# Sliding-window attention and a residual MLP on one core: every transpose of q, k and u on TensorE in place of DMA transposes

## The chip, the core and the metric

The kernel runs on one core of a Trainium2 chip. A core has five engines with instruction streams of their own: TensorE (PE, matrix products and transposes), VectorE (DVE), ScalarE (ACT), GpSimd (POOL) and SyncE (SP, which here only issues DMAs). They meet through semaphores. Data lie in SBUF (128 partitions) and, as results of TensorE, in PSUM banks. DMAs, issued from the queues of SP, ACT and POOL, move data between the device's memory and SBUF, or within SBUF. The metric is device time in microseconds (us), the median of several runs; lower is better.

## The reference

Inputs are q, k, v of shape (4, 8, 768, 64) (batch, head, position, head dimension) and the parameters of an MLP with d_model 512 and hidden width 2048.

```python
# attention: 4 sink positions and a causal window of 128
scores = scale * np.matmul(q, k.transpose(0, 1, 3, 2))
keep = is_sink | in_window
scores = np.where(keep, scores, -1000000000.0)
a = softmax(scores)
x = np.matmul(a, v)               # heads side by side: (4, 768, 512)
# residual MLP with affine norms
a1 = alpha1 * x + beta1
tok = np.einsum('ts,bsd->btd', w_tok, a1)
u = x + lam * tok
a2 = alpha2 * u + beta2
ch = np.maximum(a2 @ w_ch1, 0.0) @ w_ch2
out = u + lam * ch
```

Two transposes of data are needed in each batch. The scores contract over the head dimension, so q and k are wanted with the head dimension on the partitions. The product a2 @ w_ch1 contracts over channels, so u is wanted with channels on the partitions.

## The kernel before

The kernel works on the four batches b = 0 to 3, one after the other, with the attention of batch b + 1 woven into the MLP of batch b. A position block is 128 rows, so a batch has six (NR = 6). Heads go in pairs: four pairs (hp) with q (t = 0) and k (t = 1) of each, so a batch has eight q/k tiles.

**The order is written out.** The function describes each step as a task, `add(priority, engines, function, after, uses)`: a piece of work of one engine with what it depends on and the buffers it uses. Tables fix the rest: `ORDER` (L216) is the sequence in which all tasks are emitted, and so the order within each engine, `ENGINES` the engine of each task, `HOMES` the physical buffer, and `IDLES` a few matmuls on zeros that are set between others. An engine works its list strictly in order; a step whose input is late holds up all that stands behind it on that engine. `emit` (L54) plays the tables. The priorities and the durations in `add` play no part when the kernel runs.

**The steps of a batch**, by the names that the profile shows:

- `load_qk` (L389) loads a q/k tile into `nat`, from SP's or ACT's queue (six tiles of batch 0 from POOL's, cast on the way). For batches 0 and 1 (`b < XB`, L319) each partition gets six consecutive positions of a head, one long row (L401); for batches 2 and 3 each partition gets the same position of each block, in rows of 64 numbers (L405). `load_v` (L408) loads v.
- `trans` (L481) casts a tile to fp16 (`n`, L155 and L157) and transposes it into `qkT`. In batches 0 and 1, six matmuls of a 128 x 128 block with the identity (`tr`, L511 or L508) write into one PSUM bank (`tp`), and a copy (`ev`, L514) takes them to `qkT` and puts the positions in order. In batches 2 and 3 one DMA transpose for each tile, issued by SP, takes `n` to `qkT` (L527).
- `sinks` (L536), `scores` (L587) and `pv` (L706): the score matmuls `S` (L621), the exponential on ACT (`E`, L643), the mask on DVE or POOL, and the product with v (`pv`, L722); DVE then divides by the row sums (`rec` L747, `x` L748). `la_b` and `lb_b` are the vectors of the first affine map, each multiplied by lam once at the start (L1168).
- `tok` (L844): six matmuls of 512 columns for each position block (L853), added to x by DVE (L860), which gives u; ACT or POOL casts it to `u16`.
- u is transposed. In batch 0 `uTp` (L882) does it with two groups of six matmuls for each half of the batch (384 positions), and the affine map (alpha2, beta2) reads the result from PSUM and writes `uT` (L877 on ACT, L879 on DVE). In batches 1 to 3 `uTx` (L906) issues one DMA transpose from SP for each position block (L912), and when a half is complete, four affine steps work in place in `uT`.
- `mlp1` (L925): h, four matmuls of 384 columns for each of 16 row blocks and each half (L933), and relu on ACT or DVE (L939, L941).
- The second product is plain in batch 0 (`mlp2`, `ch`, L1118). In batches 1 to 3 it is a Strassen scheme of seven half-size products (`prod`, P1 to P7, L1050).

**Buffers.** Four PSUM banks (`d`) are shared by tok, h, ch, P, pv and all transposes; two pairs of banks (`S`) hold scores. A matmul into a bank waits until the bank's last reader is done. There is one `uT` and one `qkT`: the first step that writes those of the next batch waits for the last reader of this one.

The two DMA transposes, as they stand:

```python
        if b >= XB:
            done["qkT", b, hp, t] = add(
                p, {SP: 1340}, lambda e: nc.sync.dma_start_transpose(
                    o.t[:, 2 * hp + t, :].rearrange("p (r i) -> p r i", r=NR),
                    n16().rearrange("p r i -> p (r i)")),
                [a] + prior, [bn, o], lands=(48, 5))
            return
```

Of the kernel before, what the change touches and what calls it, by code (L numbers as in the profile page):

```python
# [77 lines left out]
def kernel(  # L78
# [17 lines left out]
    nc = tc.nc  # L96

    B, H, S, D = q.shape
    P = 128
# [98 lines left out]
    for r in range(NR):  # L198
# [18 lines left out]
        6, 7, 0, 26, 1, 10, 5, 2, 9, 11, 45, 18, 8, 19, 48, 3, 22, 15, 46, 4, 49, 12, 50,  # L217
        14, 17, 47, 13, 16, 90, 43, 103, 39, 41, 91, 28, 72, 104, 95, 53, 54, 63, 51, 42,
        73, 52, 21, 44, 74, 20, 96, 109, 100, 40, 107, 110, 65, 24, 68, 108, 92, 69, 55, 61,
        56, 93, 97, 101, 98, 59, 30, 94, 102, 111, 23, 99, 62, 113, 57, 114, 25, 112, 116,  # L220
        60, 105, 115, 58, 27, 128, 64, 106, 117, 31, 131, 135, 29, 129, 125, 132, 138, 66,
        130, 179, 78, 126, 122, 178, 140, 118, 139, 123, 197, 127, 136, 119, 137, 32, 70,
        146, 120, 141, 133, 33, 84, 79, 134, 124, 144, 147, 34, 80, 85, 71, 150, 121, 86,
        142, 75, 67, 35, 154, 143, 151, 76, 148, 158, 155, 145, 152, 77, 87, 166, 156, 159,
        81, 162, 167, 160, 88, 163, 82, 168, 89, 213, 157, 164, 83, 209, 153, 217, 149, 214,
        218, 210, 229, 219, 211, 215, 212, 226, 165, 216, 36, 230, 185, 220, 161, 177, 223,
        222, 176, 232, 221, 224, 204, 225, 175, 227, 257, 169, 237, 233, 279, 238, 199, 234,
        171, 258, 273, 280, 231, 186, 259, 228, 274, 182, 277, 172, 260, 241, 278, 174, 246,
        200, 295, 170, 248, 247, 291, 296, 37, 181, 187, 243, 293, 292, 242, 289, 198, 294,
        384, 267, 188, 290, 281, 268, 173, 271, 349, 282, 180, 285, 272, 358, 301, 351, 286,  # L230
        378, 303, 189, 203, 297, 302, 192, 304, 249, 366, 190, 379, 298, 250, 287, 369, 380,
        385, 206, 288, 283, 191, 375, 386, 367, 353, 265, 284, 368, 352, 370, 363, 376, 266,
        253, 381, 377, 371, 299, 254, 372, 615, 364, 205, 300, 382, 201, 365, 373, 275, 374,
        383, 357, 261, 276, 183, 387, 408, 262, 614, 263, 409, 202, 269, 184, 411, 410, 395,
        264, 239, 621, 617, 412, 397, 240, 270, 388, 400, 396, 235, 616, 196, 244, 398, 401,
        355, 255, 245, 236, 390, 256, 193, 359, 389, 251, 399, 207, 311, 195, 252, 391, 424,
        426, 393, 335, 392, 360, 425, 636, 312, 194, 427, 208, 336, 394, 648, 428, 413, 634,
        419, 414, 622, 404, 420, 337, 405, 429, 402, 415, 313, 422, 416, 421, 361, 441, 305,
        403, 442, 638, 423, 626, 406, 314, 640, 619, 437, 315, 430, 443, 316, 435, 431, 641,
        338, 436, 362, 618, 433, 306, 438, 649, 341, 317, 432, 407, 444, 637, 644, 307, 345,  # L240
        439, 339, 620, 318, 445, 434, 628, 635, 450, 642, 308, 451, 340, 440, 452, 639, 446,
        453, 417, 319, 447, 645, 323, 418, 320, 309, 448, 643, 658, 321, 324, 623, 449, 322,
        329, 625, 659, 454, 646, 325, 347, 647, 330, 455, 343, 326, 344, 464, 456, 465, 348,
        466, 460, 650, 457, 467, 327, 458, 331, 629, 461, 459, 462, 653, 632, 651, 463, 656,
        332, 654, 356, 472, 627, 652, 333, 342, 310, 38, 655, 660, 624, 480, 473, 468, 469,
        470, 474, 885, 665, 471, 476, 481, 475, 482, 488, 477, 350, 483, 492, 489, 478, 630,
        490, 657, 493, 479, 514, 491, 516, 328, 515, 882, 663, 518, 880, 517, 879, 498, 666,
        661, 664, 502, 499, 354, 508, 519, 512, 346, 509, 662, 678, 513, 671, 484, 679, 676,
        486, 503, 504, 487, 485, 677, 506, 877, 672, 680, 548, 507, 526, 505, 549, 334, 674,
        631, 522, 527, 907, 546, 681, 523, 633, 903, 528, 547, 534, 878, 529, 890, 675, 682,  # L250
        535, 542, 683, 689, 543, 550, 685, 690, 510, 551, 686, 494, 511, 673, 667, 544, 495,
        891, 668, 496, 545, 901, 669, 687, 497, 693, 888, 883, 897, 688, 684, 530, 694, 700,
        531, 524, 670, 696, 701, 500, 525, 552, 697, 501, 691, 698, 553, 558, 699, 695, 704,
        562, 705, 904, 692, 559, 707, 909, 563, 709, 706, 887, 564, 708, 898, 710, 702, 566,
        565, 715, 910, 567, 713, 703, 716, 532, 714, 889, 520, 533, 717, 899, 538, 537, 556,
        521, 881, 539, 884, 921, 557, 540, 536, 560, 541, 902, 718, 922, 572, 711, 574, 573,
        896, 712, 908, 576, 561, 719, 577, 575, 555, 727, 720, 569, 721, 580, 722, 728, 578,
        581, 729, 723, 905, 730, 579, 554, 739, 568, 724, 592, 740, 725, 582, 570, 911, 726,
        588, 593, 583, 912, 584, 595, 571, 743, 906, 731, 589, 732, 585, 590, 605, 733, 900,
        587, 744, 596, 745, 606, 734, 594, 607, 611, 597, 895, 602, 612, 586, 613, 599, 603,  # L260
        591, 757, 600, 759, 758, 601, 741, 765, 742, 771, 766, 760, 916, 772, 746, 751, 917,
        773, 752, 913, 886, 761, 919, 774, 604, 767, 918, 598, 762, 763, 768, 777, 764, 779,
        920, 923, 780, 914, 755, 915, 778, 608, 756, 926, 930, 735, 609, 924, 927, 931, 925,
        753, 736, 781, 737, 893, 928, 775, 782, 738, 892, 929, 934, 754, 932, 769, 610, 935,
        941, 770, 819, 776, 894, 942, 939, 820, 821, 940, 937, 936, 823, 749, 822, 748, 945,
        824, 938, 747, 827, 933, 948, 950, 750, 943, 952, 951, 825, 953, 787, 828, 944, 807,
        788, 797, 826, 808, 949, 946, 829, 954, 798, 801, 830, 791, 802, 947, 956, 792, 783,
        957, 961, 789, 784, 962, 958, 963, 955, 790, 785, 959, 964, 811, 965, 805, 812, 786,
        795, 806, 960, 967, 796, 799, 793, 968, 970, 966, 972, 794, 813, 969, 971, 815, 973,
        814, 809, 800, 974, 816, 803, 810, 976, 804, 978, 837, 975, 979, 977, 835, 838, 980,  # L270
        841, 836, 818, 839, 843, 842, 840, 981, 845, 832, 982, 846, 817, 986, 983, 844, 831,
        990, 987, 847, 991, 988, 984, 833, 855, 992, 834, 851, 993, 848, 1002, 852, 849,
        985, 998, 1003, 989, 856, 1004, 850, 859, 1005, 1006, 860, 853, 997, 868, 995, 1007,
        996, 999, 865, 1008, 858, 857, 1000, 1009, 862, 869, 866, 874, 1001, 994, 854, 1016,
        863, 875, 1040, 1017, 871, 1041, 1038, 872, 1020, 1039, 1028, 1021, 1011, 1032,
        1029, 1013, 1018, 1033, 1024, 1012, 1019, 1034, 1010, 1042, 1035, 1025, 1036, 1076,
        1037, 1043, 1070, 1077, 870, 1074, 1071, 1054, 1075, 1022, 1055, 1060, 1023, 1058,
        1061, 1048, 1014, 1049, 1059, 1066, 1015, 1044, 1067, 1072, 1045, 1056, 1073, 1026,
        1057, 1078, 1068, 1079, 1064, 1069, 1046, 1027, 1063, 1052, 1047, 1050, 1053, 1082,
        1051, 1062, 1084, 1083, 1065, 1030, 1080, 1085, 1101, 1031, 1081, 1091, 1102, 1107,  # L280
        1092, 1097, 1093, 1105, 1108, 864, 1098, 1103, 867, 1106, 1111, 1104, 1113, 1112,
        1089, 1114, 1115, 1086, 1116, 1090, 861, 1094, 1087, 1109, 1099, 1121, 1100, 1117,
        1095, 1110, 1125, 1118, 1122, 1134, 1124, 1123, 1126, 1128, 1135, 1127, 1088, 1119,
        1136, 1120, 1140, 873, 876, 1129, 1131, 1141, 1096, 1142, 1137, 1130, 1132, 1133,
        1138, 1139,
    )
    ENGINES = (
        "3313134433443333444444444444444433334443111211211212021212021203331121211210210200201210"
        "2020201202011202020202020213213213213213213202002020202020213121312131213121312131444444"
        "4444413114433334413314413314444042210221021021020121321021321202020020211212020202020212"  # L290
        "1212020212120202120212020212121202020202022221022221422221022221422221022221013111111331"
# [24 lines left out]

    V0 = (((0, 1), (2, 3), (4, 5)), ((0, 1, 2), (3, 4, 5)))

    XB = 2  # L319

    CASTING = {(0, hp, t) for hp in range(HP) for t in range(2) if hp > 0}
    QK_ORDER = [(hp, t) for hp in range(HP) for t in range(2)]
# [583 lines left out]
    def uTx(p, b, ti):  # L906
# [8 lines left out]
        if ti % 3 < 2:  # L915
            return
# [410 lines left out]
```

## Time and profile before

| | |
|---|---|
| Median of 3 runs | 254.85 us (254.72 to 255.77) |
| The profiled execution's own time | 255.22 us |
| Its span, first to last instruction | 253.4 us |
| DMA traffic | 38.79 MB in 86,129 packets, 73,540 of them under 512 B |
| Mean granted TensorE clock | 1.000 |

The profile is of one execution. Its page begins with the busy time of each engine, as time, share of the span and number of instructions; PEld are the weight loads of TensorE, which overlap with its matmuls. Then it cuts the span into 40 equal slices of 6.3 us and gives one digit for each, the busy share in tenths (9 is 90% or more); PEclk in the same manner is the clock that TensorE was granted, and DMA the mean busy share of the sixteen DMA engines. Then comes the chain of work that ended last, followed back from the last instruction, with shares of the span by engine and line. The same chain can be listed in order of time: start, length, what ran. The groups of instructions give the busy time of a kind of instruction, the mean of one in ns, and the idle time of its engine just ahead.

The stages, by the chain in order of time: scores and attention of batch 0 with the preparation of w_tok until 31.0 us; tok of batch 0 until 37.5; h of batch 0 from 41.8 (the first pieces at 39.4); ch of batch 0 from 66.8 to 97.9; h of batch 1 from 102.5; h of batch 2 from 153.0; h of batch 3 from 208.8; the last product ends near 248.9, and the stores of the output end the span.

### The profile page before, as it was taken

The page shows a single profiled execution, that of the slowest core. Times are in us where ns is not written, and L with a number is a line of the kernel's source. Part 1 is how long each engine was busy: PE and PEld are TensorE (multiplying, and loading weights), DVE is VectorE, ACT ScalarE, POOL GpSimd, SP SyncE. Part 2 cuts the span into 40 slices and gives each one's busy share as a digit, 9 for nine tenths or more (in the row PEclk, how much of TensorE's full clock was granted, in tenths as well). Part 3 has the DMA queues.
Part 4 walks back from the last instruction along what each step waited for, and adds up shares of the span by engine and source line. Part 5 has one row for each costly group of instructions (what it writes and reads, how often), then busy time and mean ns, then how long its engine had stood idle before and what let it go on. Part 6 is the DMA issues. An engine that isn't in the chain of part 4 may idle for free.

```text
span 253.4 us, 5513 instructions
## 1 busy us (share of the span) xinstructions
PE 245.6 (97%) x2167; PEld 160.4 (63%) x2167; DVE 193.6 (76%) x401; ACT 131.4 (52%) x218; POOL 107.7 (42%) x126
## 2 busy tenths in 40 slices
PE   8799999999999999999999999999999999999992
PEld 8654655675555544566777786577577676667882
DVE  6898987778798876688889986677789985029882
ACT  2389935688986025687750536556560234643000
POOL 8708903987866516443772040066462130000010
PEclk9999999999999999999999999999999999999999
DMA  7999999999999997896489274320000131100317
GB/s 208 200 256 349 218 205 300 369 350 275 218 195 224 211 198 162 168 257 141 107 179 186 41 155 128 124 65 0 3 0 3 31 73 23 41 0 3 137 54 268
DMA packets 86129, 38.79 MB, mean 153 GB/s; under 512 B 73540, under 2 KB 80460, under 8 KB 86104
## 3 DMA queue, kind: packets, MB, share of 16 engines
q1 hardware_dynamic: 67120, 28.85, 48.4%
q10 hardware_dynamic: 15240, 6.32, 10.3%
q0 software_dynamic: 3744, 3.28, 8.2%
q8 instruction: 17, 0.28, 0.5%
q14 instruction: 8, 0.07, 0.1%
HBM read 29.91 MB, written 6.29 MB: 143 GB/s over the span
## 4 chain that ended last, share of the span: by engine, by line
PE 89%; ACT 4%; DVE 4%; issue 2%; DVEq 0%; ACTq 0%
PE h L933 32%; PE P L1050 22%; PE tok L853 12%; PE ch L1118 8%; PE pv L722 4%; PE S L621 4%; PE idle L148 2%; PE tp L511 1%; ACT wt L818 1%; ACT E L643 1%; DVE qkT L157 1%; DVE lb_b L1168 1%; PE S L616 1%; PE tp L508 1%; PE pv L715 1%
## 5 line engine op out<-in xcount | busy, mean ns | idle before, releaser
L933 PE MATMUL h<-uT,w1f 128*128 128x384 f16 x512 | 89.5, 326 | 0.4 <-DVE x L860 0.3
L933 PEld LDWEIGHTS <-w1f 128*128 128x128 f16 x512 | 48.3, 98 | 32.5 <-issue 2.2
L939 ACT ACTIVATE hT<-h 128x384 f16<-128x384 f32 x77 | 36.7, 493 | 34.8 <-PE h L933 31.1
L941 DVE TENSOR_SCALAR hT<-h 128x384 f16<-128x384 f32 x51 | 27.4, 553 | 24.0 <-PE h L933 23.6
L1050 PEld LDWEIGHTS <-hT 128*128 128x128 f16 x408 | 39.3, 98 | 6.9 <-DVE hT L993 0.6
L643 ACT ACTIVATE E<-S 128x1024 f16<-128x1024 f32 (+1 forms) x39 | 37.9, 1002 | 6.9 <-PE S L621 5.9
L766 POOL TENSOR_TENSOR tm<-x,la_b 128x512 f32<-128x512 f32 x18 | 24.7, 1372 | 22.3 <-DVE x L748 11.2
L853 PE MATMUL tok<-xh,wtokT 128*128 128x512 f16 x144 | 33.2, 379 | 0.0
L1050 PE MATMUL P<-w2f,hT 128*128 128x256 f16 x216 | 26.7, 273 | 0.0
L155 ACT CAST u<-x 128x512 f16<-128x512 f32 x17 | 10.3, 617 | 27.9 <-DVE x L860 26.8
L1063 DVE TENSOR_TENSOR x<-x,P 128x256 f32<-128x256 f32 x45 | 18.1, 417 | 7.2 <-PE P L1050 6.6
L1086 POOL TENSOR_TENSOR x<-x,pt 128x256 f32<-128x256 f32 x4 | 4.0, 995 | 46.0 <-DVE pt L1081 46.0
L1050 PE MATMUL P<-w2s,hT 128*128 128x256 f16 x192 | 23.2, 273 | 0.0
L853 PEld LDWEIGHTS <-wtokT 128*128 128x128 f16 x144 | 13.8, 98 | 14.7 <-issue 0.2
L1118 PE MATMUL ch<-w2f,hT 128*128 128x512 f16 x96 | 22.7, 379 | 0.0
L748 DVE TENSOR_TENSOR x<-pv,rec 128x256 f32<-128x256 f32 x48 | 20.4, 425 | 1.7
L155 ACT CAST n<-nat 128x768 f16<-128x768 f32 x20 | 16.2, 830 | 8.6 <-DVE vs L575 6.7
L860 DVE TENSOR_TENSOR x<-x,tok 128x512 f32<-128x512 f32 x24 | 16.0, 682 | 4.6 <-PE tok L853 4.4
L722 PEld LDWEIGHTS <-E 128*128 128x128 f16 x328 | 15.2, 97 | 4.9 <-issue 1.1
L722 PE MATMUL pv<-vfs,E 128*128 128x65 f16 x328 | 17.7, 193 | 0.0
L583 POOL TENSOR_SCALAR_AFFINE_SELECT E<-E 128x512 f16<-128x512 f16 x12 | 8.8, 757 | 17.6 <-ACT E L643 17.6
L157 POOL CAST vfs<-vnat 128x512 f16<-128x512 f32 x18 | 13.5, 751 | 4.2 <-PE pv L722 4.2
(133 smaller groups left out, 340.4 us busy)
## 6 DMA issues: line engine op xcount, KB each, us to landing
wst_w<-in_moe_w_ch_dram SPq DMA_DIRECT2D x8, 512.0 KB, 7.4
nat<-in_q_dram SPq DMA_DIRECT2D x10, 384.0 KB, 4.1
nat<-in_k_dram SPq DMA_DIRECT2D x10, 384.0 KB, 7.9
vnat<-in_v_dram SPq DMA_DIRECT2D x14, 256.0 KB, 5.8
out_dram<-x SPq DMA_DIRECT2D x11, 256.0 KB, 2.8
out_dram<-x ACTq DMA_DIRECT2D x10, 256.0 KB, 3.8
wtn<-in_moe_w_tok_dram SPq DMA_DIRECT2D x6, 384.0 KB, 4.8
w1f<-in_moe_w_ch_dram POOLq DMA_DIRECT2D x4, 512.0 KB, 13.5
```

The lines of the kernel that those rows point to most:

```text
L155: nc.scalar.copy(o, i)
L643: nc.scalar.activation(eT.t, pS.t[:, :, 0 : n * w].rearrange("p e (i w) -> p e i w", i=n), AF.Exp, scale=scale)
L722: nc.tensor.matmul(po.t[:, hl, :], eT.t[:, e_, off + i, c : c + P], vf[j][:, h, :], start=(r < 2 and n == 0), stop=(n == len(parts) - 1 an ...
L748: nc.vector.tensor_mul(bx.t[:, 4 * G : 4 * G + 4, :], po.t[:, :, 0:D], rec.t.to_broadcast([P, 4, D]))
L766: engine[e].tensor_mul(bt.t, bx.t.rearrange("p h d -> p (h d)"), la1_b)
L853: nc.tensor.matmul(pt.t, wtokT[:, si, ti * P : (ti + 1) * P], hs[si].t, start=(si == 0), stop=(si == NR - 1))
L933: nc.tensor.matmul(ph.t, w1f[:, c, fi * P : (fi + 1) * P], bu.t[:, c, chk * NTOK : (chk + 1) * NTOK], start=(c == 0), stop=(c == NC - 1))
L939: nc.scalar.activation(bh.t[:, fi, :], ph.t, AF.Relu)
L941: nc.vector.tensor_scalar_max(bh.t[:, fi, :], ph.t, 0.0)
L1050: nc.tensor.matmul(pc.t, hh[:, nt * P : (nt + 1) * P], w(fi), start=(first and n_ == 0), stop=(n_ == HF - 1), skip_group_check=True)
L1063: nc.vector.tensor_add(row(bx)[:, cols], row(bx)[:, cols], pc.t)
L1118: nc.tensor.matmul(pc.t, bh.t[:, fi, nt * P : (nt + 1) * P], w2f[:, fi, :], start=(fi == 0), stop=(fi == NF - 1))
```

## The change

All transposes of q, k and u go through TensorE. The branch with the DMA transpose in `trans` and the whole of `uTx` are taken out; batches 2 and 3 go through `tr` and `ev` as batch 1 does, and batches 1 to 3 call `uTp` after the third and the sixth tok block. The rows of q and k of batches 2 and 3 are loaded as those of batches 0 and 1, six positions to a partition. The tables ORDER, ENGINES and HOMES are new throughout; IDLES is as it was.

```diff
-    XB = 2
...
-        if b < XB:
-            src = src.rearrange("h (p r) d -> p h (r d)", p=P)
-            done["nat", b, hp, t] = add(
-                p, {SP: 480, ACT: 550}, lambda e: queue[e].dma_start(bf.t, src), [wait], [bf], lands=(16, {(0, 0, 1): 85, (0, 1, 0): 140}.get((b, hp, t), 68)))
-        else:
-            src = src.rearrange("h s d -> (h s) d").rearrange("(x p) d -> p x d", p=P)
-            done["nat", b, hp, t] = add(
-                p, {SP: 630, ACT: 600}, lambda e: queue[e].dma_start(
-                    bf.t.rearrange("p e (r d) -> p (e r) d", r=NR), src), [wait], [bf], lands=(96, 18))
+        src = src.rearrange("h (p r) d -> p h (r d)", p=P)
+        done["nat", b, hp, t] = add(
+            p, {SP: 480, ACT: 550}, lambda e: queue[e].dma_start(bf.t, src), [wait], [bf], lands=(16, {(0, 0, 1): 85, (0, 1, 0): 140}.get((b, hp, t), 68)))
...
-        if b >= XB:
-            done["qkT", b, hp, t] = add(
-                p, {SP: 1340}, lambda e: nc.sync.dma_start_transpose(
-                    o.t[:, 2 * hp + t, :].rearrange("p (r i) -> p r i", r=NR),
-                    n16().rearrange("p r i -> p (r i)")),
-                [a] + prior, [bn, o], lands=(48, 5))
-            return
         pt = Buf("d", [P, S], FP16, f"tp{b}_{hp}_{t}")
         a = add(p, {PE: 336}, tr, [a, wait, done["iden"]], [bn, pt], mode="col" if direct else None)
         done["qkT", b, hp, t] = add(p + 0.1, evac, ev, [a] + prior, [pt, o])
...
-    def uTx(p, b, ti):
...
-        done["uTd", b, ti] = add(
-            p, {SP: 1315}, lambda e: nc.sync.dma_start_transpose(
-                bo.t[:, :, ti * P : (ti + 1) * P], bu.t),
-            [done["u16", b, ti]], [bu, bo], lands=(48, 5))
...
-            if b and what == "tok":
-                uTx(p + 0.3, b, *args)
+            if b and what == "tok" and args[0] % 3 == 2:
+                for cp in range(2):
+                    uTp(p + 0.3, b, args[0] // 3, cp)
...
-                    trans(p if nb < XB else w0 - 15 + i, nb, hp, t, {POOL: 775, ACT: 735}, {DVE: 880, ACT: 695},
-                          wait=done["tok", b, 2])
+                    trans(p if nb == 1 else w0 - 15 + i, nb, hp, t, {POOL: 775, ACT: 735}, {DVE: 880, ACT: 695},
+                          wait=done["tok", b, 2] if nb == 1 else None)
```

What the new tables make of each engine's list, against the one before:

| Engine | Before | After |
|---|---|---|
| PE, transposes of q and k into `tp` (not those of batch 0's cast loads) | 60 | 156 |
| PE, transposes of u | 24 | 96 |
| ACT, copies `qkT` from `tp` | 7 | 23 |
| ACT, affine of u from SBUF / from PSUM | 15 / 4 | 0 / 16 |
| DVE, affine of u from SBUF / from PSUM | 9 / 4 | 0 / 16 |
| ACT / POOL, casts of q and k | 20 / 4 | 18 / 6 |
| ACT / POOL, casts of u | 17 / 7 | 16 / 8 |
| DVE / POOL, scaling of w_ch2 by lam | 7 / 9 | 4 / 12 |
| DVE / POOL, the product lb_b | 1 / 0 | 0 / 1 |
| SP, DMA transposes | 34 | 0 |

At the start of the lists, POOL issues the first two of its q/k loads ahead of four small mask steps, DVE casts k of the first pair before q and both before the two bias steps, ACT takes the exponential of score block 1 before that of block 2, and the product lb_b stands behind the first v cast on POOL. In batches 2 and 3 the eight groups of q/k transposes are set among ch and pv of batch 0, and among P and tok of batches 1 and 2. The groups for u stand one to four PE tasks behind the tok blocks that they need.

## The prediction

> **What bounds the kernel now.** I read the page's busy shares and the slices first, then the chain of waits, then the chain in order of time, and last the rows of the instructions that the change touches.
>
> ```profile
> span 253.4 us, 5513 instructions
> ...
> PE 245.6 (97%) x2167; PEld 160.4 (63%) x2167; DVE 193.6 (76%) x401; ACT 131.4 (52%) x218; POOL 107.7 (42%) x126
> ...
> PE   8799999999999999999999999999999999999992
> ...
> PEclk9999999999999999999999999999999999999999
> DMA  7999999999999997896489274320000131100317
> ...
> PE 89%; ACT 4%; DVE 4%; issue 2%; DVEq 0%; ACTq 0%
> ```
>
> The reader is to see that TensorE (PE) fills 97% of the span, that it makes up 89% of the chain, and that its clock is full in every slice. DMA is a different matter: it is full in the first third and idle in the later slices, and PE does not notice.
>
> A busy PE need not be a full PE, so I count. From 43.87 us (the last transposes of batch 0's u begin) to 248.86 us (the last vector add) lie 205.0 us. Pitches come from the chain in order of time: h 0.1625 us a matmul (116 in 18.85), tok 0.2156 (18 in 3.88), the products P 0.1093 (152 in 16.61), ch 0.216 (12 in 2.59), a score matmul 0.0675 (8 in 0.54), pv 0.030 (8 in 0.24), a transpose 0.057 (below). What the stretch holds is 488 h (79.3), 108 tok (23.3), 504 P (55.1), 96 ch (20.7), the scores of three batches (8.9), pv and its sink part (10.5), the sink scores and vsp (1.7), 60 transposes (3.4): 202.9 us. **Slack is 2.1 us in 205.** Before 43.87 us it is otherwise: there ScalarE (ACT) and VectorE (DVE) carry the chain between PE's pieces.
>
> **What the change takes off.** All 34 DMA transposes go:
>
> ```profile
> L912 SPq DMA_TRANSPOSE uT<-u x18: 1188/1198/1267, 94.0 to 208.0; - x18
> ...
> L527 SPq DMA_TRANSPOSE qkT<-n x16: 1210/1282/2468, 77.4 to 148.7; - x16
> ```
>
> Their columns are shortest, median and longest issue in ns. They occupy SP's queue for 18 x 1.198 + 16 x 1.282 = 42.1 us, beside PE. In the list of PE's waits, the longest is 1.1 us, and no DMA is named. So removing them is worth nothing on the path. The same holds for the 16 loads of q and k of batches 2 and 3 in long rows: less DMA time, in a place where nothing on the path waits for a load. Stores and v loads that stood behind the transposes on SP go earlier, and nothing on the path waits for those either; ACT issues 6 of the 16 loads before and after, about 0.4 us each.
>
> **What it adds on PE.** 16 groups of six transposes for q and k (8 a batch in batches 2 and 3) and 12 groups of six for u (4 a batch in batches 1 to 3): 28 groups, 168 matmuls. Batch 1's own transposes, interleaved with h as the new ones will be, show the price:
>
> ```profile
> 52.41 0.34 PE tp L511 x6
> 52.74 0.65 PE h L933 x4
> 53.39 0.34 PE tp L511 x6
> 53.73 0.65 PE h L933 x4
> 54.38 0.34 PE tp L511 x6
> 54.71 0.65 PE h L933 x4
> 55.36 0.73 PE tp L511 x12
> 56.09 1.30 PE h L933 x8
> 57.40 1.00 PE tp L511 x18
> ```
>
> Eight groups take 2.75 us, 0.34 each, or 0.057 a transpose, and h keeps its 0.65 for four beside them. 28 x 0.342 = **9.6 us**, all in the stretch with 2.1 us of slack, so on the path. The group table gives 219 ns as the mean of one, but that is a latency that overlaps the next; 168 x 219 = 36.8 us is the upper end, excluded by the pitch.
>
> Two rules of the Trainium skill, "TensorE: Matmul & The Clock Gate". Its section "Back-to-back issue gap" states about 81 ns sustained for weight load and matmul at 128 columns: 168 x 81 = 13.6 us (an estimate from that page), 4 us more than the row's 9.6. The row is of this kernel and this very operation, so I take it. Its "Part 4: PE-mode transpose" speaks against the change more strongly: transposes do not count as PE activity for the clock, so more of them might cost speed around them. The row: in 50 to 60 us, with 48 transposes in it, the granted clock was 1.00. The new order never puts more than two groups (0.7 us) together. By the row: 0; by the rule, unknown and above 0.
>
> **Evacuations.** Each q/k group needs a copy from PSUM: 16 more on ACT (7 become 23), 0.80 us each in the row of such copies: 12.8 us. The affine of u now reads PSUM: on DVE 0.477 instead of 0.372 us, on ACT 0.669 instead of 0.697. There were 15 on ACT and 9 on DVE from SBUF; now 12 and 12 from PSUM: ACT -2.4, DVE +2.4 us. Some small steps change engine (three w2 scalings and two casts of q/k to POOL, three steps off ACT altogether). In sum ACT comes to about 140 us, DVE to 192, POOL to 114, of some 263: none becomes the bound. What hides the copies is PE's other work, if the PSUM bank is free in time. There are four "d" banks. Counting PE's work by the pitches between a new group and the next user of its bank, the shortest is 0.99 us (a u group, whose two halves go to ACT and DVE side by side), and most q/k groups have 1.1 to 1.3 us. A copy of 0.80 with its hops fits, with 0.1 to 0.3 to spare; without that cover each group costs what the copy is late.
>
> **Waits that the change adds.** PE now stands in line at a u group until the u casts are done, with the next score, ch or P matmuls behind it. From tok's end the path is DVE add 0.68 and cast 0.62 with hops, about 1.5 us. Between the tok and the first u group of batch 1 the new order has 1.7 us of PE work, the least of all; others have 1.8 to 3.9. The q/k groups wait for their casts, last done at 89.8 us before, and the last group of batch 2 stands near 93. Bounds: 0, or 0.3 us for half of the 28 groups, 4 us; no wait removed here is on the path, so no gain. Nearest row: the eight groups at 52 us, which waited for nothing. I take 0.4 us.
>
> **The head.** "Steps set anew" leaves PE and ACT in nearly the same order here. One piece matters:
>
> ```profile
> 8.29 0.95 DVE qkT L157
> 9.24 1.89 DVE lb_b L1168
> 11.13 0.87 DVE wt L820 x2
> 12.00 0.88 DVE qkT L157
> ```
>
> The product lb_b stands on the path, ahead of a copy of k that the first full score waits for. It moves to POOL, which sat idle from 12.4 to 18.7 us. The ends are 0 and -1.9 us. What is late next: the copy of q of the same pair, on ACT, ended at 12.37 (0.5 us before DVE's 12.88), and one more exponential (0.60) now stands ahead of it, in time that ACT spent idle (0.66). So the gain is 0.5, not 1.9, and from 14 us on ACT has no gap over 0.3 us until tok. The first casts now come k before q, ahead of two bias steps; PE's 67 idle matmuls cover that until 6.4 us. I take **-0.5**.
>
> **Sum.** 253.4 + 9.6 + 0.4 - 0.5 = 262.9 us span; the execution's own time was 255.22, 1.8 above its span, so 264.7; the median of the three runs is 0.37 below that execution: **264.4 us**.
>
> **Rivals.**
> *The head pays back, the slack swallows.* All of lb_b's 1.9 us comes off, because ACT's copy is not late, and half of the slack takes transposes: 9.6 - 1.9 - 1.0 = 6.7, 261.5 us. For it: lb_b is on the chain. Against: ACT's copy.
> *The banks bind.* An ACT instruction (an exponential is 1.02 us) stands ahead of a copy, the bank comes back 0.5 us late, for 12 of the 28 groups: 9.6 + 6 - 0.5, 270 us. For it: only 0.1 to 0.3 us to spare, all 16 copies on ACT. Against: ACT is busy 0.2 to 0.5 of the time where most groups lie (80 to 100 us, 130 to 160 us).
> *Not slower.* PE's busy time is modelled, and matmuls could wait inside it; transposes then fill those holes. It decides once the slack after 43.87 us is 9.6 - 1.9 = 7.7 us: 254.8 us. My count gives 2.1, so I can give this almost nothing. The VectorE page of the skill ("VectorE: DVE Perf Modes", rules for kernel authors) would side with it: it prefers TensorE for a 128x128 transpose if PSUM will do, at 390 ns against 1309 by DMA. By that rule the change saves; by the rows the cheaper engine is the full one, and the dearer one stands idle.
> *The change doesn't do what it says:* the built order has the 168 transposes and no DMA transpose, so this falls away.
>
> **Chances.** Forecast 0.70 (its own range 262.8 to 266.3), head pays back 0.12, banks 0.15, not slower 0.02, the rest beyond these. The range 261.5 to 268.0 takes in the second case and the milder half of the third. A measurement of this kernel can tell about 0.5%, 1.3 us, from no change: slower 0.97, within 0.02, faster 0.01.
>
> **What would show it.** Transposes of 0.34 a group, PE's share still 97%, h 0.65 for four. Batch 1's first h (102.5 us before) comes 10 groups later, less the head: 105.4 + the small waits. Batch 2's first h (153.0) stands 22 groups later, +7.0; batch 3's (208.8) all 28, +9.1. ACT near 140 us. Wrong would be: gaps of PE before or after new groups (banks, casts), a clock under 1.00, or tok beginning more than a microsecond before 31.0 us.

## The result, and the profile after

The changed kernel takes **268.77 us** (median of 4 runs, 268.41 to 268.84), beside 255.00 us for the kernel before on the same chip (254.72 to 255.77). The ratio, with its 95% interval, is **1.0532 [1.0507, 1.0558]**: 5.3% slower. The forecast was 264.4 with a range to 268.0; the direction was right, and 4.4 us are missing from the sum.

The page of the changed kernel, the same lines as were shown of the one before:

```profile
span 267.0 us, 5782 instructions
...
PE 257.7 (97%) x2335; PEld 171.1 (64%) x2335; DVE 195.0 (73%) x402; ACT 139.9 (52%) x227; POOL 113.0 (42%) x132
...
PE   8899999999999998999999999999999999999993
...
PEclk9999999999999999999999999999999999999999
DMA  7999999999286308337430007010000000100217
...
PE 86%; ACT 6%; DVE 5%; issue 2%; ACTq 0%; DVEq 0%
```

PE is as full as before, 97% of a longer span, at a full clock. The other engines have about the loads that the prediction worked out (ACT 140, POOL 114; DVE, put at 192, has 195). But PE's share of the chain fell from 89 to 86%, and ACT and DVE took more: PE now waits for somebody.

The 13.6 us that the span grew by fall into three parts:

| Part | How it is read | us |
|---|---|---|
| head, to the long h piece of batch 0 | starts at 42.38, before at 41.76 | +0.6 |
| 168 transposes on PE | 28 groups of 0.34 in the chain in order of time | +9.5 |
| new waits, from there to the last vector add | 220.05 us (42.38 to 262.43) against 207.10 (41.76 to 248.86), less 9.5 | +3.5 |

So the big term was right, and what fails lies in the two small ones. Of the 3.5 us, 2.1 are idle time of PE: in this stretch it is busy for 217.86 of the 220.05 us, in the kernel before for 206.98 of 207.10. The other 1.4 stand inside its busy time, and by an estimate most of them belong to the pauses too: four h matmuls with a pause behind them keep PE busy for 0.81 us (from 110.43 in the list of instructions), against 0.65 where others follow at once, and PE pauses nine times in this stretch, before once; 8 x 0.16 are 1.3. Where the gaps lie, the chain of the changed kernel in order of time tells (start, length, what ran; pieces of 0.1 us and less are left out), here around the first half of batch 1's u and then around the second:

```profile
99.68 0.56 PE S L608 x8
100.27 1.02 ACT E L630
101.38 0.61 ACT uT L864
102.02 0.49 DVE uT L866
102.55 2.89 PE tok L840 x12
...
108.71 0.46 PE uTp L881 x6
109.19 0.68 ACT uT L864
109.93 0.36 issue
110.29 0.48 DVE uT L866
110.79 0.68 ACT uT L864
111.52 4.06 PE h L901 x24
```

The reader is to see that the two affine halves of a u group do not run at the same time. They read the same PSUM tile, one engine `pt[:, 0]` and the other `pt[:, 1]`. In the first place DVE begins at 102.02, 0.03 us after ACT's end, and only when DVE is done is the bank free for the tok block at 102.55; in the second, ACT begins at 110.79, 0.02 us after DVE's end, ahead of h at 111.52. So it is in all fourteen groups that this kernel splits between the engines: the later half waits for a semaphore that the earlier half raises. That both also write one tile, `uT`, is not the reason: in the kernel before, ACT's affine in `uT` runs from 100.31 to 101.01 us and DVE's begin at 100.42. Why the program sets the wait for a shared PSUM tile no run here shows. So in the first place a u group holds its bank for an exponential in front of ACT's half (1.02), then 0.67 and 0.48 in a row.

The lists of waits say the same. First those of PE, then one line of those of DVE (who waited, for whom: us in total, times, longest):

```profile
PE tok L840 <- DVE uT L866: 0.7, 1, 0.7
PE h L901 <- DVE uT L866: 0.5, 2, 0.3
PE P L1018 <- DVE x L847: 0.4, 1, 0.4
```

```profile
DVE uT L866 <- ACT uT L864: 7.5, 8, 2.8
```

DVE works its list in order, so while it stands in line for ACT (7.5 us in all, up to 2.8 at once) everything behind it is late too; in the chain, the wait of P for DVE's x (219.24 us) goes back over six steps of DVE to such a half at 215.65.

### The profile page after: what moved, and what is told of

Read it like the earlier page. It is cut to its first block, busy times and chain, and to the rows that moved or that the text cites. A ratio compares the mean times of both kernels' runs of the same rounds, so it can differ in the third digit from the quotient of the medians.

```text
span 267.0 us, 5782 instructions
## 1 busy us (share of the span) xinstructions
PE 257.7 (97%) x2335; PEld 171.1 (64%) x2335; DVE 195.0 (73%) x402; ACT 139.9 (52%) x227; POOL 113.0 (42%) x132
## 4 chain that ended last, share of the span: by engine, by line
PE 86%; ACT 6%; DVE 5%; issue 2%; ACTq 0%; DVEq 0%
PE h L901 30%; PE P L1018 19%; PE tok L840 11%; PE ch L1086 7%; PE pv L709 4%; PE S L608 3%; PE tp L505 3%; PE idle L148 3%; ACT uT L864 2%; ACT E L630 2%; PE uTp L881 1%; DVE uT L866 1%; ACT wt L805 1%; DVE qkT L157 1%; PE pv L702 1%
## 5 line engine op out<-in xcount | busy, mean ns | idle before, releaser
L155 ACT COPY qkT<-tp 128x768 f16<-128x768 f16 x23 | 18.3, 799 | 14.5 <-PE tp L505 14.5
L1054 POOL TENSOR_TENSOR x<-x,pt 128x256 f32<-128x256 f32 x4 | 3.4, 852 | 46.5 <-DVE pt L1049 46.5
L155 ACT CAST u<-x 128x512 f16<-128x512 f32 x16 | 9.7, 618 | 23.5 <-DVE x L847 23.1
L822 POOL TENSOR_TENSOR w2f<-wst_w,lam_b 128x512 f16<-128x512 f32 x12 | 16.5, 1392 | 0.0
L864 ACT ACTIVATE uT<-uTp,ab 128x384 f16<-128x384 f16 x16 | 10.2, 670 | 10.7 <-PE uTp L881 9.7
```

What stands on the lines that cost most here:

```text
L155: nc.scalar.copy(o, i)
```

## The experiments

The runs go by the first part of their names, e1 to e11. The theories that the expectations name: **A**, the serial halves of the u groups make the gaps. **B**, the q/k groups' copies on ACT bring their banks back late. **C**, the new order is worse throughout, whoever it is that waits. Later, for the head: **D**, PE's 67 matmuls on zeros ("fillers") last too long and hold the first transposes; **E**, the head is held by its casts, copies or loads. Unless another is named, the kernel that is edited is the changed one. Ratios are to the kernel before, on the same chip. The runs come from several chips, on which the kernel before had medians of 254.88 to 255.41 us, so a difference of two medians from different chips is good to about 0.5 us.

### One engine for both halves of a u group

```diff
                 lambda e, ci=ci, c=c: affine(
-                    e, bo.t[:, c, chk * NTOK : (chk + 1) * NTOK], pt.t[:, ci, :], c),
+                    (ACT if cp else DVE) if b else e, bo.t[:, c, chk * NTOK : (chk + 1) * NTOK], pt.t[:, ci, :], c),
```

> The changed kernel with one edit: in batches 1 to 3 both halves of a group of u go to one engine, the first group's to ACT, the second group's to DVE (12 and 12 steps, as before). Theory A (the halves wait for each other across engines, DVE for ACT, and this holds banks and DVE's list): the 3.5 us of new PE gaps shrink by more than half, 266.0 us (265.3 to 267.3). Theory B (the q/k copies on ACT come late for their banks) and theory C (the new order is worse throughout): 268.8 us, no change.

Measured: 267.13 us (266.02 to 267.63), ratio 1.0463 [1.0425, 1.0501]. That is 1.6 us less than the changed kernel, for an edit that moves no work on PE. The two profiles have the same head (h of batch 0 at 42.38), and from there to the last add this one takes 1.4 us less. So the time is in A's range, but of the 3.5 us less than half went. Two waits for u were left, tok 0.7 and h 0.3 us, both for ACT's affine: the group transposed first had come to ACT, which had an exponential in front. The swap takes that away (`DVE if cp else ACT`):

> The changed kernel with both affine halves of a u group on one engine, as in e1_u_one_engine, but the first group of each pair on VectorE and the second on ScalarE (there it was the other way round). In the one before, TensorE still waited 0.7 us (a tok block) and 0.3 us (h) for the affine on ScalarE, which stood behind an exponential. Theory A (what costs is a u group's bank coming back late, by the chain of its two halves): the first group's bank comes back from VectorE in 0.95 us, the second has 0.9 us more time; both waits go, 267.13 - 1.0 = 266.1 us (265.4 to 266.8). Theory C (the gaps belong to the new order as such, and only change their name): 267.1 us or more.

Measured: 266.66 us (266.43 to 267.12), ratio 1.0433 [1.0395, 1.047], 2.1 us less than the changed kernel and within the range that A gave. The chain at the same place:

```profile
99.16 0.56 PE S L608 x8
99.74 1.02 ACT E L630
100.86 1.15 ACT uT L864 x2
102.01 0.92 ACT E L630
102.96 1.09 DVE E L645
104.05 0.61 DVE x L847
104.70 0.29 PE pv L709 x4
```

No wait of PE names uT any more, and tok follows at 101.18 without a gap. But the next exponential on ACT still stands behind two affines, DVE's mask waits for it, the add of x behind the mask holds a bank, and pv waits:

```profile
PE pv L709 <- DVE x L847: 0.8, 1, 0.8
```

From the h of batch 0 (41.85) to the last add (260.17) this kernel takes 218.3 us, 1.7 less than the changed one: so of the 3.5 us, **1.7 go with the serial halves**. (The rest of the 2.1 is a head that was 0.5 us shorter, with fillers that ended sooner.) Of the other 1.8, 0.8 is this new wait and 0.3 are shorter gaps of PE; the rest stands in PE's busy time, and no run took it apart.

### u by DMA transposes, in the changed order

Each u cast of batches 1 to 3 issues a DMA transpose from SP, the u groups on PE are empty, and the affine works in place in SBUF, as before.

```diff
...
         def uc(e):
             copy(e, bu.t, bx.t.rearrange("p h d -> p (h d)"))
+            if b:
+                bo = uT[b, 0]
+                plan.hold(bo)
+                nc.sync.dma_start_transpose(bo.t[:, :, ti * P : (ti + 1) * P], bu.t)
...
```

> The changed kernel with u of batches 1 to 3 back on DMA transposes (one for each block, issued by SP once its cast is written), affine in place in SBUF; q and k stay on TensorE. Theory A: 12 groups of 0.34 and most of the 3.5 us of gaps go, 268.8 - 4.1 - 3 = 261.7 us (261.0 to 262.7). Theory B: only the 4.1 us go, 264.7. Theory C: 264.7 or more.

Measured: 274.98 us (274.43 to 275.29), ratio 1.0781 [1.0755, 1.0806]: 13 us above A, 10 above B, and only the open end of C ("264.7 or more") takes it in. ACT stood in line for the DMAs, and with it what PE needed:

```profile
ACT uT L873 <- DMA uT<-u: 19.5, 6, 4.5
```

The changed order puts the affine close behind the casts, which suits a group of TensorE transposes that takes 0.34 us; the DMA transposes were waited for up to 4.5 us in it. So this kernel says nothing on A, B or C; it shows that here the path could not be exchanged without the order.

### q and k of batches 2 and 3 by DMA transposes

```diff
...
         def tr(e):
+            if b >= 2:
+                plan.hold(o)
+                nc.sync.dma_start_transpose(
+                    o.t[:, 2 * hp + t, :].rearrange("p (r i) -> p r i", r=NR),
+                    n16().rearrange("p r i -> p (r i)"))
+                return
...
```

The copy from PSUM falls away too, and the loads are in short rows again; all else stays as changed.

> The changed kernel with q and k of batches 2 and 3 back on DMA transposes and short rows, set where TensorE's groups stood; u stays on TensorE. Theory A: 16 groups of 0.34 go and the gaps stay, 268.8 - 5.5 = 263.3 us (262.6 to 264.3). Theory B: the gaps go with the copies, 268.8 - 5.5 - 3 = 260.3. If SP's issue comes late for the sink scores, later than 264.3.

Measured: 264.48 us (263.81 to 264.62), ratio 1.0366 [1.0341, 1.0391]. It is 4.3 us faster than the changed kernel, and 0.2 above A's range; for the sink scores, which the last case names, PE has no wait in the list. 16 groups of 0.34 are 5.5 us. The saving is less than their PE time: a wait of P of 0.6 and three of 0.2 us came in their place. Had their copies held banks as B has it, the saving would have been more, so B falls. The waits on u stay (tok, h), and the new one of P is for u too:

```profile
PE tok L859 <- DVE uT L885: 0.7, 1, 0.7
PE P L1037 <- DVE uT L885: 0.6, 1, 0.6
PE h L920 <- DVE uT L885: 0.5, 2, 0.3
```

### The kernel before, with batch 1's q and k by DMA transposes as well

The same edit with `b >= 1` in the kernel before. It also puts the loads of batch 1 in short rows. It asks whether the eight groups that PE still does there could be saved.

> The kernel before, carried one step further: q and k of batch 1 by DMA transposes too, in short rows, at the places of the TensorE groups. If a transpose on a full PE costs its pitch whoever else is idle: 8 groups of 0.34 go, 255.0 - 2.7 = 252.3 us (251.8 to 253.2). If the DMA engines, full between 40 and 65 us, deliver the short rows or the transposes late: 255 us or more, with PE waiting for scores of batch 1 near 60 us.

Measured: 277.3 us (275.92 to 278.09), ratio 1.0868 [1.0828, 1.0909], 22 us slower for taking work off the full engine. In its waits:

```profile
PE h L947 <- ACT hT L953: 14.8, 2, 13.7
...
ACT n L160 <- DMA qkT<-n: 13.3, 1, 13.3
```

A cast on ACT waited 13.3 us for a DMA transpose to give its buffer back, the relu of h stood behind that cast, and PE behind the relu. That is the second case of the expectation, though PE stood mostly at h and not at the scores (4.3 us). From 50 to 70 us the mean busy share of the DMA engines, as the profile counts it, was over 1 (1.19), PE was busy for 6.3 of the 20 us, and its granted clock was 0.80 and then 0.50; the q/k transposes landed in 3.7 us in the median, against 2.8 in the kernel before. Whether the short rows or the transposes filled the DMA engines is not told apart. Here a DMA transpose was free only where the DMA engines had room and nothing in an in-order list stood behind it.

### Every new transpose twice

```diff
-            for r in range(NR):
+            for r in list(range(NR)) * (2 if b > 1 else 1):
...
-            for ci in range(2):
+            for ci in [0, 1] * (2 if b else 1):
```

> The changed kernel with the six transposes of each of the 28 new groups done twice (168 more matmuls, same result, nothing else). By the pitch of 0.057 us, with nothing to hide it: 268.8 + 9.6 = 278.4 us (277.6 to 279.4). By 81 ns a transpose: 282.4 us. If part of the added transposes goes into gaps where TensorE waits: below 277 us. If the extra work makes banks or casts late: above 279.4 us with new waits of TensorE.

Measured: 275.56 us (275.34 to 275.95), ratio 1.0781 [1.0738, 1.0825]: 6.8 us more than the changed kernel, not 9.6, and far from 282.4, which the 81 ns of the page that the prediction names would make. It is the case of transposes that go into gaps. The chain in order of time shows that the price holds:

```profile
136.50 0.87 PE P L1018 x8
...
137.72 0.67 PE tp L505 x12
138.39 0.87 PE P L1018 x8
...
139.62 0.67 PE tp L505 x12
```

Twelve transposes take 0.67 us, so 28 x 0.335 = 9.4 us were added. From the h of batch 0 (41.39) to the last add (269.0) are 227.6 us, 7.6 more than in the changed kernel. The other 1.8 us went into pauses: PE's idle time there is 0.9 us, not 2.2, and the 0.7 us in front of tok and the 0.5 of h for DVE's uT are gone from its waits. That is a second witness for the gaps, by filling them. (Its head was 1.0 us shorter than in the changed kernel's profile, from which the next runs start.)

### The head: fillers and lb_b

At the start PE runs 67 fillers until the first casts are done. Their row in the kernel before, in the changed kernel, and in the kernel before with lb_b moved (e8):

```profile
1.06 5.35 PE L148 MATMUL idle<-warm 128*128 128x128 f16 x67 [1.06 <-DVE warm L174]
6.55 0.83 PE L511 MATMUL tp<-iden,n 128*128 128x128 f16 x12
```

```profile
1.06 6.70 PE L148 MATMUL idle<-warm 128*128 128x128 f16 x67 [1.06 <-DVE warm L174]
7.91 0.83 PE L505 MATMUL tp<-iden,n 128*128 128x128 f16 x12
```

```profile
1.06 6.74 PE L148 MATMUL idle<-warm 128*128 128x128 f16 x67 [1.06 <-DVE warm L174]
7.95 0.83 PE L511 MATMUL tp<-iden,n 128*128 128x128 f16 x12
```

The same 67 matmuls last 5.35 or 6.7 us, and the first transposes stand behind them. Each kernel has one profile, so how far this length varies between executions of one kernel is not known. The next runs take fillers away, in the swapped kernel (e6), the changed one (e11) and the kernel before (e10), always by the same edit:

```diff
-        (46, 0, 67), (90, 1, 25), (109, 3, 2), (166, 1, 4), (162, 0, 1),
+        (46, 0, 46), (90, 1, 25), (109, 3, 2), (166, 1, 4), (162, 0, 1),
```

> The kernel of e5_u_swap with 46 in place of 67 matmuls on zeros at the start. Theory D (the head lost 0.6 us because those matmuls lasted until 7.77 us, beyond the casts that were done at 6.40): the first transposes begin near 6.6 instead of 7.9 us, and the time falls by 0.7 to 1.3 us against e5. Theory E (the head is held by its casts and copies on VectorE, or the matmuls that are left run at half their rate for longer[...]): the same as e5 within 0.3 us, or up to 0.5 us slower.

Measured: 265.73 us (265.56 to 266.86), ratio 1.0402 [1.0363, 1.0441], 0.9 us below e5 on the same chip, within D's range; the first transposes begin at 6.62, tok of batch 0 at 30.36 (the list of instructions in order of time has it at 31.47 in the changed kernel and at 30.85 in the one before).

> The changed kernel with 46 in place of 67 matmuls on zeros at the start, nothing else. Theory D: 268.8 - 0.9 = 267.9 us (267.5 to 268.3), tok of batch 0 near 30.4 us in place of 31.6, 0.6 us ahead of the kernel before, which would be the gain that the prediction gave to the head. Theory E: 268.8 us.

Measured: 267.71 us (267.38 to 268.11), ratio 1.0484 [1.0466, 1.0501], 1.06 us below the changed kernel, tok at 30.56, 0.9 us earlier: D, for the changed kernel.

> The kernel before with 46 in place of 67 matmuls on zeros at the start. In its profile they lasted 5.35 us and the cast of q was done at 5.85, but in a profile of the same list with lb_b moved they lasted 6.74 us. Theory D (how long they last differs from run to run, because the rate doubles at a time that the kernel does not set, and where they last long they hold the first transposes): 0.3 to 1.0 us faster, 254.1 to 254.8 us, and less spread. Theory E (the head is held elsewhere, or TensorE is slow for longer): 254.9 us or slower.

Measured: 255.61 us (253.81 to 257.48), ratio 1.0012 [0.9988, 1.0036]: nothing gained, and more spread. Its first transposes began at 5.74 us, 0.8 earlier than in the kernel before, and its tok at 30.27, 0.6 earlier. But e4, whose list has the same head and 67 fillers (5.63 us), had its tok at 30.27 as well, with first transposes at 6.84; so fewer fillers bring nothing there, and the 0.6 has another cause (below, the product lb_b). In e10 PE waited 0.8 us for a late load of q at 15.89. Behind the head, it waited for a v cast of batch 1 on POOL, and that cast for a load:

```profile
68.40 0.37 PE L722 MATMUL pv<-vfs,E 128*128 128x65 f16 x7 [1.12 <-POOL vfs L157]
...
67.73 0.61 POOL L157 CAST vfs<-vnat 128x512 f16<-128x512 f32 x1 [2.12 <-DMA vnat<-in_v_dram]
```

The profiled execution took 257.1 us, one of the slowest of the 14, so this last wait need not be in the others. D holds for the changed kernel and E for the one before.

The product lb_b alone, in the kernel before (the third edit of the next diff):

> The kernel before with the product lb_b on GpSimd instead of VectorE, all else as before. The prediction's step: -0.5 us, 254.4 us. If nothing is late next: -1.9 us, 253.0 us. If it was hidden anyway: 254.9 us.

Measured: 255.19 us (254.52 to 255.87), ratio 0.9987 [0.9969, 1.0005]. The 1.9 us of DVE time are worth 0.2 us by the medians, which the interval does not tell from nothing. Its one profile cannot decide it, because its fillers lasted 1.4 us longer (tok at 31.38). But the 1.9 us are themselves one execution's. The same product in the kernel before and in e10:

```profile
9.16 1.97 DVE L1168 TENSOR_TENSOR lb_b<-lb_b,lam_r 128x512 f32<-128x512 f32 x1
```

```profile
8.35 0.74 DVE L1168 TENSOR_TENSOR lb_b<-lb_b,lam_r 128x512 f32<-128x512 f32 x1
```

In e4 it takes 0.94 us: it begins 0.3 us later there than in the kernel before (9.45), and what follows it on DVE begins 0.7 earlier (10.32 against 11.05). It meets the product la_b on POOL each time: before it began 0.4 us after that one, in e4 0.9 us after it, and in e10 0.2 us ahead of it, where POOL's took 1.67 us in place of 1.3. That the two hold each other up fits these times; no run tests it.

The last one takes the kernel before with 46 fillers, lb_b on POOL, and one engine for each u group of batch 0:

```diff
-        (46, 0, 67), (90, 1, 25), (109, 3, 2), (166, 1, 4), (162, 0, 1),
+        (46, 0, 46), (90, 1, 25), (109, 3, 2), (166, 1, 4), (162, 0, 1),
...
-                    e, bo.t[:, c, chk * NTOK : (chk + 1) * NTOK], pt.t[:, ci, :], c),
+                    ACT if cp else DVE, bo.t[:, c, chk * NTOK : (chk + 1) * NTOK], pt.t[:, ci, :], c),
...
-            a = add(p, {DVE: 635, POOL: 1220}, lambda e, o=o: engine[e].tensor_mul(o, o, lam_r),
+            a = add(p, {DVE: 635, POOL: 1220}, lambda e, o=o: engine[POOL].tensor_mul(o, o, lam_r),
```

> The kernel before with three small edits: 46 matmuls on zeros, lb_b on GpSimd, and in batch 0 both affine halves of a u group on one engine (VectorE for the first group, ScalarE for the second). If all three add up: 46 fillers -0.3 to -1.0, lb_b -0.2, the wait of 0.28 us of VectorE for ScalarE -0.3: 253.4 to 254.1 us. If only the fillers count: as e10. If none does: 254.9 us.

Measured: 255.56 us (253.94 to 257.19), ratio 1.0003 [0.9978, 1.0029]. Its profiled execution had a span of 251.9 us, 1.5 below the kernel before, but the longest of the others had 255.0. Its tok began at 29.74, earlier than in any other profile, which the median does not show. No version here beats the kernel before.

## Why the prediction was wrong, point by point

- **What bounds the kernel: right.** PE stayed at 97%, and 34 DMA transposes taken away gave nothing that can be seen. The run with q and k on DMA transposes (e3) gives the cleanest view of the choice: 4.3 us faster than with those 96 transposes on PE.
- **Price of the transposes: right.** 9.6 predicted, 9.5 found, 0.335 a group in the doubled kernel. The 81 ns that "TensorE: Matmul & The Clock Gate", "Back-to-back issue gap", would have given (13.6 us) were rightly left aside for the row of this kernel: 0.67 us for twelve are 56 ns. Of the loss around transposes that its "Part 4" gave reason to fear nothing was seen: the granted clock stayed at 1.00 (mean 0.999), and at 1.00 with the transposes doubled, and h kept its 0.65 us for four between them. No stretch of transposes here is longer than 1.3 us. The rule of "VectorE: DVE Perf Modes" that prefers TensorE fails here, as argued: it does not ask which engine is full, and 4.3 us came back when q and k left it.
- **Evacuations: the step that failed.** It said that the bank of a u group is free in time because its "two halves go to ACT and DVE side by side". They go one after the other. By the rows of the prediction itself, ACT 0.669 and DVE 0.477 make 1.15 us with the hops on top, against a shortest free time of 0.99; the comparison would have come out negative. The wait was to be seen in the kernel before, where the first half of batch 0 does the same thing, in its chain in order of time:

```profile
37.91 1.24 ACT uT L877 x2
39.18 0.48 DVE uT L879
39.66 0.59 DVE x L860
```

  There too DVE begins when ACT's half of the group has ended. The prediction looked at the in-place affines of batch 1, which do overlap, and at the durations, not at the starts. The rival "the banks bind" had the right kind of mechanism and the wrong place: it put the lateness on the copies of q and k, for which PE never waits in the list (e3 has the same waits for u without them).
- **Waits that the change adds: mis-sized.** 0.4 was taken, the new waits come to 3.5. The bounds (0 to 4 us) held it, but the nearest row was badly chosen: the eight groups at 52 us are q/k groups with one copy by one engine, and say nothing of a group with two readers. Of the 3.1 us that are missing here, 1.7 are the serial halves (e5); the rest stays open.
- **The head: wrong in sign.** It was put at -0.5 and came out at +0.6 in the profile. "PE's 67 idle matmuls cover that until 6.4 us" took their length of one execution for a fixed one. In the changed kernel's profile they ran to 7.77, and by the medians (e11) fewer fillers give 1.06 us back. The gain was misread in the same way: the 1.9 us of lb_b on DVE, from which it was worked out, are 0.74 in e10 and 0.94 in e4. So the order is not shown to gain anything. With fillers alike, tok begins no earlier than in the order before: with 46 at 30.56 (e11) against 30.27 (e10), with 67 that last 6.7 us at 31.47 against 31.38 (e8, lb_b moved).
- **The sum.** 3.1 us of waits and 1.1 of the head are 4.2 of the 4.4 that are missing.
- **The checkpoints** showed it: the first h of batch 1 was forecast at 105.4, of batch 2 at 160.0, of batch 3 at 217.9; they came at 106.9, 162.5 and 222.0. Less the 1.1 us by which the head missed, the distance is 0.4, 1.4 and 3.0 us: it grows from batch to batch and is not a loss at the start alone. With both causes mended (e6) the kernel takes 265.73, 1.3 us above the forecast (0.7 by the ratios to the kernel before on the same chip), and these stay open.

## What to carry to other kernels

Before two engines are counted as reading a PSUM tile side by side, look in the trace for one pair that does, by start times: here the second reader always stood behind the first, and giving each tile to one engine, the first tile to the engine that is free sooner, won 1.7 us in the stretch behind the head without touching the work. On a kernel whose PE has 2 us of slack in 205, a transpose belongs on whichever path is idle, and the DMA path serves only where the order leaves time for the landing: moved without lead it cost 6 us (e2) and 22 us (e4). A filler loop is part of the path as soon as it outlasts what it covers. And a length that is read off one profile, of fillers or of a product on DVE, can be another in the next: a term of half a microsecond should not rest on one.

## What the runs showed of the hardware that was not expected

- PE's rate at the start doubles at a time that differed between profiles with the same fillers in front. Fillers go at one per 0.107 us at first (8 in 1.06 us, each 0.31) and then at one per 0.056 (13 in 0.89, each 0.22); the change came near 4.1 us in the profile of the kernel before and after 6.5 us in e8, so that 67 lasted 5.35 to 6.74 us. The profile's granted clock reads 1.00 throughout, so this is seen in counts by stretch alone, and a granted clock of 1.00 is no proof of the full rate. What sets the time was not found.
- The DMA transposes of q and k, landing in 2.8 us in the median in the kernel before, took 5.6 us in e3, though they were issued over the same time (77.5 to 147.9 us, before 77.4 to 148.7); their landing time is no constant of the instruction. The cause was not found.
- The product lb_b on DVE took 0.74, 0.94 or 1.97 us in three profiles (e10, e4, before), as it met a product on POOL at one moment or another.
- A transpose added between other matmuls costs the same 0.056 us whether six or twelve stand together, and part of it vanishes where PE waits anyway (e7: 9.4 us added, 7.6 seen).
